# A zeroed tile shared on GpSimd, one VectorE instruction folded, and six semaphores taken back by SyncE in the kernel's ending

## The chip, the cores and the metric

The kernel runs on one core of a Trainium2 chip. The time is the device time in microseconds (us). A kernel was executed three times or more on one chip, in rounds shared with the kernel before. Absolute times of different chips are not compared closely: ratios are of the same rounds.

The **span** runs from the first to the last instruction of the kernel in the trace. **Time minus span** is what is counted beyond it. Exact spans (to a nanosecond) come from the one profiled execution of a kernel. For its other executions the span is known to 0.1 us.

## The reference, cut to what matters

One token through attention over a window of 4096 cached keys and values, a dense GELU layer, and a gate between the two:

```python
def reference(A_x, A_k_cache, A_v_cache, A_wq, A_wo, B_x, B_w1, B_b1, B_w2, B_b2, gate_w):
    x = A_x
    g = _sigmoid((x * gate_w).sum(-1, keepdims=True))
    a = _A_ref(x, A_k_cache, A_v_cache, A_wq, A_wo)     # 32 query heads, 16 key heads, Dh = 128
    b = _B_ref(x, B_w1, B_b1, B_w2, B_b2)               # 576 -> 4608 -> 576
    return g * a + (1 - g) * b
```

Every weight and cached value is read once, 53.6 MB in all.

## The kernel before: the parts concerned

GpSimd makes constants at the opening, each with a memset and one or more selections:

```python
    perm = const.tile([P, 4, 4, 32], BF16, name="perm")
    nc.gpsimd.memset(perm[:], 0.0)
    nc.gpsimd.affine_select(out=perm[:], in_=perm[:], ...)            # cut
    hi5 = const.tile([P, 5], FP32, name="hi5")
    nc.gpsimd.memset(hi5[:], 1.0)                                     # two selections follow, cut
    lo31 = const.tile([P, RW], BF16, name="lo31")
    nc.gpsimd.memset(lo31[:], 0.0)
    for a in range(5):
        nc.gpsimd.affine_select(out=lo31[:], in_=lo31[:], pattern=[[-1, RW]], ..., base=-RW * a, ...)
    om_t = const.tile([P, 64], BF16, name="om_t")
    nc.gpsimd.memset(om_t[:], 0.0)
    wo_tail = const.tile([48, 4, D], BF16, name="wo_tail")
    nc.gpsimd.memset(wo_tail[:].bitcast(FP32), 0.0)
```

VectorE scales the softmax sums (`rgh` for four columns, `rgt` for the fifth), and TensorE folds the heads with `lo31`:

```python
    nc.vector.tensor_tensor(out=rgh[:], in0=rg[:].to_broadcast([P, Hq, 4]), in1=gh[:, :, 0:4]..., op=ALU.mult)
    nc.vector.tensor_scalar(out=rgt[:], in0=rg[:, :, 0], scalar1=gh[:, 0, 4:5], ...)
    # cut
    ov_mm = nc.tensor.matmul(ov_ps[:, 0:RO], lhsT=om[:]..., rhs=lo31[:], start=True, stop=True)
```

The ending is written by the kernel itself. SyncE issues the store, arrives at the kernel's barrier, waits until the store has landed and takes its semaphore back to zero. GpSimd waits for the loads' semaphores and four arrivals, then clears the other semaphores as two ranges:

```python
        last = copy.replace(leave, sync_info=mybir.SyncInfo(on_wait=[landed], on_update=[taken]))
        kept = [arrive, last]                  # SyncE: arrive, then wait for the store and take back
        # ACT, PE and DVE arrive, cut
        kept += [copy.replace(ours[0], sync_info=others), ours[1]]   # GpSimd: others' waits; 4 arrivals
        # two range clears, (lo, sem) and (sem + 1, hi), cut
```

## Time and profile before

| | before |
|---|---|
| time, median of the first three executions | 132.34 us (132.33 to 132.4) |
| span of the profiled execution | 130.28 us |
| its time | 132.28 us, so time minus span is 2.00 us |
| one load queue, share of 16 engines | 96.5% |

How to read it: the busy shares (TensorE 62%, VectorE 41%, GpSimd 8%) are no guide here, as the load queue is nearly always full. One looks for what can starve that queue, and for what stands behind its last byte. The prediction below shows the DMA rows and the end of the chain. The lines here are those that the parts of the change touch.

GpSimd's opening, from the timeline (start, length, engine, line, operation):

```profile
9.89 0.74 POOL L226 TENSOR_SCALAR_AFFINE_SELECT perm<-perm 128x512 bf16<-128x512 bf16 x1
10.76 1.05 POOL L271 MEMSET wo_tail<- 48x1152 f32 x1
...
14.79 1.56 POOL L291 TENSOR_SCALAR_AFFINE_SELECT foreign<-foreign 4x512 bf16<-4x512 bf16 x1
16.33 0.21 POOL L259 TENSOR_SCALAR_AFFINE_SELECT lo<-lo 128x31 bf16<-128x31 bf16 x1
16.50 0.99 POOL L384 MEMSET qz_flat<- 128x1084 f32 x1
```

GpSimd is done with its last constant at 17.5 us; nothing of it runs later but the ending.

VectorE at the softmax sums, same view; the bracket gives the idle time before an instruction and what ended it:

```profile
105.28 0.36 DVE L633 RECIPROCAL rg<-mt_ps 128x32 f32<-128x32 f32 x1 [15.54 <-PE mt_ps L628]
105.68 0.29 DVE L635 TENSOR_TENSOR rgh<-rg,gh 128x128 f32<-128x128 f32 x1
105.89 0.23 DVE L642 TENSOR_SCALAR rgt<-rg,gh 128x32 f32<-128x32 f32 x1
114.89 0.29 DVE L661 TENSOR_TENSOR om<-o_ps,rgh 128x128 bf16<-128x128 f32 x1 [8.76 <-PE o_ps L603]
```

After `rgt` VectorE idles for 8.76 us. An instruction fewer here saves no waiting.

TensorE behind the folding products, and the very end:

```profile
121.89 2.61 PE L359 MATMUL y_ps<-wo_t,ov 128*1 128x288 bf16 x40 [0.19 <-DMA wo_t<-in_A_wo_dram]
125.35 1.39 PE L359 MATMUL y_ps<-w_t,gt 128*1 128x288 bf16 x20 [0.85 <-DMA w_t<-in_B_w_dram]
...
128.62 0.45 DVE L702 CAST out_row<-y_ps 1x288 bf16<-1x288 f32 x1 [11.72 <-PE y_ps L359]
129.12 0.28 SPq L703 DMA_DIRECT2D out_dram<-out_row  x1
```

TensorE waits for loads three times in the last 10 us (0.19, 0.85 and, at 127.44, 0.33 us), so a product more is taken in. The store's issue at 129.12 us is the last thing that these views show.

### The profile page before, as it was taken

To read this page: it belongs to the slowest core of one execution; us is meant where nothing else is said; L and a number is where in the kernel's file an instruction comes from. 1 tells how busy PE (TensorE), PEld (TensorE's weight loads), DVE (VectorE), ACT (ScalarE), POOL (GpSimd) and SP (SyncE) were. 2 spreads that over 40 slices of the span, in tenths; PEclk is the share of its full clock that TensorE was granted. 3 is DMA by queue.
4 is the path that set the end of the run, shared out by engine and by line. 5 is a ranking of instruction groups with operands and counts; after the bars stand their busy time and mean duration, and the time that the engine had idled before them with its cause. 6 is when DMAs were issued, how large, how long until landed. Compare 5 with 4: busy or idle time off the path is not lost.

```text
span 130.3 us, 2411 instructions
## 1 busy us (share of the span) xinstructions
PE 80.7 (62%) x1145; PEld 46.1 (35%) x1077; DVE 53.7 (41%) x49; ACT 8.3 (6%) x18; POOL 10.1 (8%) x34
## 2 busy tenths in 40 slices
PE   0036999476003998949909995985300930899973
PEld 0036949475000121202201121685300920864641
DVE  0056100300079969999999995604000020010001
ACT  3000000003000000030003003021000000000001
POOL 5029930000000000000000000000000000000000
PEclk9999999999999999999996899975555555555999
DMA  7999999899999899899999999899999999999980
GB/s 232 421 436 439 468 401 498 363 463 438 392 448 463 372 453 483 372 443 473 392 433 463 412 412 463 376 444 473 397 423 448 423 407 421 430 427 421 403 354 25
DMA packets 2508, 53.75 MB, mean 413 GB/s; under 512 B 286, under 2 KB 290, under 8 KB 580
## 3 DMA queue, kind: packets, MB, share of 16 engines
q1 hardware_dynamic: 2490, 53.61, 96.5%
q8 instruction: 8, 0.13, 0.4%
q10 hardware_dynamic: 10, 0.01, 0.0%
HBM read 53.62 MB, written 0.00 MB: 412 GB/s over the span
## 4 chain that ended last, share of the span: by engine, by line
DMA 52%; DVE 24%; PE 14%; issue 6%; SPq 2%
DMA k_t<-in_A_k_cache_dram 27%; DMA w_t<-in_B_w_dram 25%; DVE kt L494 19%; PE s_ps L516 7%; PE o_ps L603 5%; DVE m L532 3%; DVE pt L565 2%; PE y_ps L359 1%; SPq L651 1%; DVE mr L535 1%; SPq L658 0%; SPq L194 0%; PE mt_ps L541 0%; DVE out_row L702 0%; SPq L190 0%
## 5 line engine op out<-in xcount | busy, mean ns | idle before, releaser
L516 PE MATMUL s_ps<-kt,qz_flat 128*128 128x512 bf16 x128 | 32.6, 412 | 17.2 <-DVE kt L494 10.4
L494 DVE STREAM_TRANSPOSE kt<-k_t 128x4096 f32<-128x4096 f32 x8 | 35.3, 4432 | 11.7 <-DMA k_t<-in_A_k_cache_dram 10.3
L603 PE MATMUL o_ps<-pt,v_t 128*128 128x8 bf16 x512 | 14.2, 167 | 16.8 <-DMA v_t<-in_A_v_cache_dram 14.8
L516 PEld LDWEIGHTS <-qz_flat 128*128 128x128 bf16 x64 | 6.8, 107 | 40.3 <-issue 40.2
L603 PEld LDWEIGHTS <-v_t 128*128 128x128 bf16 x512 | 14.1, 102 | 17.5 <-DMA v_t<-in_A_v_cache_dram 15.1
L387 PEld LDWEIGHTS <-w_t 128*128 128x128 bf16 x162 | 10.2, 165 | 0.9 <-issue 0.9
L387 PE MATMUL h_ps<-x,w_t 128*128 128x2 bf16 x162 | 10.4, 202 | 0.0
L359 PE MATMUL y_ps<-w_t,gt 128*1 128x288 bf16 x72 | 7.2, 363 | 1.2 <-DMA w_t<-in_B_w_dram 1.2
L553 ACT ACTIVATE p_t<-s_ps,negm 128x1024 bf16<-128x1024 f32 x4 | 4.5, 1113 | 50.9 <-DVE negm L549 50.9
L633 DVE RECIPROCAL rg<-mt_ps 128x32 f32<-128x32 f32 x1 | 0.4, 358 | 15.5 <-PE mt_ps L628 15.5
L565 DVE STREAM_TRANSPOSE pt<-p_t 128x1024 bf16<-128x1024 bf16 x4 | 4.9, 1224 | 2.7 <-ACT p_t L553 2.7
L425 PE MATMUL q_ps<-x,wq_t 128*128 128x2 bf16 x144 | 4.0, 166 | 2.7 <-DMA wq_t<-in_A_wq_dram 2.7
L702 DVE CAST out_row<-y_ps 1x288 bf16<-1x288 f32 x1 | 0.4, 445 | 11.7 <-PE y_ps L359 11.7
L308 PE MATMUL xs_ps<-one_b,rows 1*128 1x1 bf16 x9 | 0.7, 195 | 7.4 <-DVE rows L302 7.4
L532 DVE TENSOR_REDUCE m<-s_ps 128x1 f32<-128x1024 f32 x4 | 4.8, 1196 | 1.1 <-PE s_ps L516 1.1
L359 PEld LDWEIGHTS <-gt 128*1 128x1 bf16 x72 | 3.7, 99 | 3.6 <-issue 1.6
L425 PEld LDWEIGHTS <-wq_t 128*128 128x128 bf16 x144 | 3.9, 104 | 2.8 <-DMA wq_t<-in_A_wq_dram 2.8
L396 DVE COPY hacc<-h_ps 128x36 f32<-128x36 f32 x1 | 0.2, 196 | 10.6 <-PE h_ps L387 10.6
L359 PE MATMUL y_ps<-wo_t,ov 128*1 128x288 bf16 x62 | 4.3, 286 | 0.2 <-DMA wo_t<-in_A_wo_dram 0.2
L661 DVE TENSOR_TENSOR om<-o_ps,rgh 128x128 bf16<-128x128 f32 x1 | 0.3, 292 | 8.8 <-PE o_ps L603 8.8
L302 DVE COPY rows<-rows 1x1152 bf16<-1x1152 bf16 x1 | 0.7, 748 | 6.5 <-DMA rows<-in_A_x_dram 6.5
L359 PEld LDWEIGHTS <-ov 128*1 128x1 bf16 x62 | 2.6, 83 | 1.8 <-issue 0.8
(77 smaller groups left out, 39.1 us busy)
## 6 DMA issues: line engine op xcount, KB each, us to landing
k_t<-in_A_k_cache_dram SPq DMA_DIRECT2D x4, 4096.0 KB, 31.8
v_t<-in_A_v_cache_dram SPq DMA_DIRECT2D x4, 4096.0 KB, 23.2
wq_t<-in_A_wq_dram SPq DMA_DIRECT2D x1, 4608.0 KB, 25.8
w_t<-in_B_w_dram SPq DMA_DIRECT2D x1, 2880.0 KB, 14.2
w_t<-in_B_w_dram SPq DMA_DIRECT2D x1, 2592.0 KB, 23.1
w_t<-in_B_w_dram SPq DMA_DIRECT2D x1, 2304.0 KB, 8.1
wo_t<-in_A_wo_dram SPq DMA_DIRECT2D x1, 2304.0 KB
wo_t<-in_A_wo_dram SPq DMA_DIRECT2D x1, 2160.0 KB
```

What stands on the lines that cost most here:

```text
L302: nc.vector.tensor_copy(out=xdup.rearrange("p (d t) -> p d t", t=2), in_=x_row.rearrange("p (d o) -> p d o", o=1).to_broadcast([1, D, 2]),)
L359: last = nc.tensor.matmul(y_out[s], lhsT=vec, rhs=row[:, s * DH : (s + 1) * DH], start=start, stop=stop, skip_group_check=True,)
L387: nc.tensor.matmul(h_ps[:, j:NF:NJ], lhsT=w1_t[:, i, j:FH:NJ], rhs=x2[:, i, :], start=False, stop=(i == NI - 1 and j == NJ - 1), skip_grou ...
L425: nc.tensor.matmul(q_ps[:, j : Hq : Hq // 2], lhsT=wq_t[:, i, j * Dh : (j + 1) * Dh], rhs=x2[:, i, :], start=(i == 0 and j == 0), stop=(i ...
L494: lambda: nc.vector.transpose(out=kt[g, f][:].bitcast(FP32), in_=keys.rearrange("p c d -> p (c d)").bitcast(FP32),),
L516: last = nc.tensor.matmul(s_ps[g][:, u * 512 : (u + 1) * 512].rearrange("p (c k) -> p c k", k=32), lhsT=qz(g, j, 2 * f + half), rhs=kv[:, ...
L532: queue("dve", lambda: nc.vector.reduce_max(out=m1[:], in_=s_ps[g][:], axis=AX.X))
L535: lambda: nc.vector.tensor_scalar(out=mr[:], in0=hi16[:], scalar1=m1[:, 0:1], scalar2=None, op0=ALU.mult),
L553: nc.scalar.activation(out=p_t[:].rearrange("p c k -> p (c k)"), in_=s_ps[g][:], func=ACT.Exp, bias=negm[:, 0:1], scale=SCALE, accum_out=s ...
L565: lambda: nc.vector.transpose(out=pt[:, g, :, :].rearrange("p c q -> p (c q)"), in_=p_t[:].rearrange("p c k -> p (c k)"),),
L603: last = nc.tensor.matmul(o_ps[:, 8 * g : 8 * g + 8, 0], lhsT=v_t[g][:, c, :], rhs=pt[:, g, c % 32, 8 * (c // 32) : 8 * (c // 32) + 8], st ...
L651: nc.sync.dma_start(out=wo_t[:, r0:r1, :].rearrange("p r n -> p (r n)"), in_=wo_src[:, 0 : 4 * RW, :].rearrange("h (a r) n -> h a (r n)", ...
```

## The change

Intent: GpSimd zeroes one tile and cuts `perm`, five selections (now side by side, one instruction), `om_t` and `wo_tail` out of it. VectorE makes `rgh` five columns wide and drops `rgt`. TensorE adds up four products where `lo31` needed one. In the ending SyncE takes six semaphores back while its store flies, so GpSimd needs to wait for three arrivals only, and clears six semaphores where it cleared eleven (five of SyncE's six were among these).

```diff
+        first = min(w.id for w in store.sync_info.on_wait)
+        mine = [w for w in waits if w.id >= first and w.id != sem]
+        mine.append(...)                       # PE's semaphore, its value counted from the program; cut
+        mine.append(next(w for w in waits if w.id == sem))
+        waits = [w for w in waits if w.id < first]
-        kept = [arrive, last]
+        kept = []
+        for w, name in zip(mine, names):       # six: wait for w, take it back; no arrival
+            kept.append(copy.replace(leave, name=name, sync_info=mybir.SyncInfo(on_wait=[w], on_update=[taken])))
-        kept += [copy.replace(ours[0], sync_info=others), ours[1]]
+        kept += [copy.replace(ours[0], sync_info=others), copy.replace(ours[1], sync_info=three)]
-        for n, (a, b) in enumerate(((lo, sem), (sem + 1, hi))):
+        for n, (a, b) in enumerate(((lo, first), (stop, hi))):
 ... (cut)
-    perm = const.tile([P, 4, 4, 32], BF16, name="perm")
-    nc.gpsimd.memset(perm[:], 0.0)
+    zeros = const.tile([P, NZ + 4 * D], BF16, name="zeros")
+    nc.gpsimd.memset(zeros[:].bitcast(FP32), 0.0)
+    # perm, at31, om_t and wo_tail are parts of zeros; one selection fills at31 (cut)
-    nc.gpsimd.memset(hi5[:], 1.0)
-    # lo31: memset and five selections; memsets of om_t and wo_tail (cut)
 ... (cut)
-    rgh = const.tile([P, Hq, 4], FP32, name="rgh")
+    rgh = const.tile([P, Hq, 5], FP32, name="rgh")
-    rgt = const.tile([P, Hq], FP32, name="rgt")
-    nc.vector.tensor_scalar(out=rgt[:], in0=rg[:, :, 0], scalar1=gh[:, 0, 4:5], ...)
 ... (cut)
-    ov_mm = nc.tensor.matmul(ov_ps[:, 0:RO], lhsT=om[:]..., rhs=lo31[:], start=True, stop=True)
+    for a in range(4):
+        ov_mm = nc.tensor.matmul(ov_ps[:, 0:RO], lhsT=om[:]..., rhs=at31[:, a, :], start=(a == 0), stop=(a == 3))
```

## The prediction

> **What bounds the kernel now.** I read the page's slices first, then the queues, the chain of work that ended last, and the timeline of the last microseconds; after that the semaphore records that the trace keeps beside the instructions, because the change is about semaphores and no page counts those as work.
>
> ```profile
> DMA  7999999899999899899999999899999999999980
> GB/s 232 421 436 439 468 401 498 363 463 438 392 448 463 372 453 483 372 443 473 392 433 463 412 412 463 376 444 473 397 423 448 423 407 421 430 427 421 403 354 25
> ...
> q1 hardware_dynamic: 2490, 53.61, 96.5%
> ```
>
> The last four pieces of the chain that ended last (start, length, what):
>
> ```profile
> 94.31 33.08 DMA w_t<-in_B_w_dram
> 127.39 0.04 issue
> 127.44 1.19 PE y_ps L359 x16
> 128.62 0.43 DVE out_row L702
> ```
>
> The DMA row is at 8 or 9 tenths in every slice from the second to the last but one, and one queue is busy for 96.5% of sixteen engines' span. So the run is one unbroken load of 53.6 MB with a tail behind it. The second fence ends in that tail: the last products, then the two copies of the result.
>
> Does any load wait for GpSimd or VectorE work? The loads' issue times against their sizes answer it. When VectorE lets the third value block be issued, at 79.60 us, the earlier issues add up to 36,960 KB, or 37.8 MB. At the mean of 413 GB/s, 79.6 us have moved 32.9 MB. So 4.9 MB, 12 us of transfer by my estimate, are still queued; the other late issues leave more (6.5 MB at 86.47 us). **No engine that is made 2 us quicker or 1 us slower in the middle moves the end of the stream.** What is left is what stands behind the last byte.
>
> **The end, from the trace's records.** The last load's semaphore is complete at 128.07 us, and the copies end at 129.04 (ScalarE) and 129.06 (VectorE). SyncE issues the store from 129.12 to 129.40, arrives at the kernel's own barrier at 129.67, and takes the store's semaphore back at 130.28, because the store has landed at 130.25. GpSimd waits for four arrivals, the last being SyncE's at 129.67, passes at 129.71, clears two ranges of semaphores, and ends at 130.09. The span ends there with SyncE, at 130.28, yet the profiled run is counted at 132.28 us. The missing 2.0 us are in the records of semaphore 2: nine increments at 128.903, 129.231, 130.621, 130.666, 130.689, 130.786, 130.826, 130.860 and 130.906[...], then nine more increments from 131.715 to 132.072.
>
> [...] two rounds of nine increments, steps of 23 to 98 ns where nobody is late, and ranges of 51 (54 to 104, 105 to 155, 156 to 206). [...] The increment at 128.903 can only be TensorE's, which alone had ended by then. [...] The range 105 to 155 is zeroed in groups of four every 21 to 22 ns, the rhythm in which GpSimd clears 99 to 109 inside the kernel (129.903, 129.925, 129.946). So **the third position is GpSimd**, and SyncE is the fifth.
>
> Read so, the first round says who is late: positions 4 and 5 follow the third by 45 and 23 ns, exactly as in the second round (44 and 24 ns), so they had been ready. The program's end now waits for GpSimd, which reports 0.527 us after its last clear (130.621 minus 130.094), and not for SyncE, although SyncE's is the last instruction of the span.
>
> [...] Here, on the hardware queue, issue to landing of the store is 1.13 us (129.12 to 130.25)[...]. [...] On GpSimd [...] 1084 fp32 in 991 ns and 512 bf16 in 522 ns, 0.91 and 1.02 ns each. So zeroing bf16 through a 4-byte view halves the cost.
>
> **The change part by part.**
>
> *GpSimd's opening.* Removed are the memsets of perm (0.52 us), lo31 (0.13), om_t (0.15), wo_tail (1.05) and hi5 (0.11) and five selections of lo31 (5 x 0.21 = 1.05): 3.0 us. Added are one memset of 1518 4-byte elements (1518 x 0.91 = 1.4 us) and one selection of 155 columns (estimate from perm's: 0.745 x 155/512 = 0.23, say 0.3 us). Net about 1.3 us of GpSimd work gone; and as the large memset runs before 9.05 us, where GpSimd idles for 6.7 us, qz_flat may be ready some 2 us sooner than 17.5 us. TensorE waits for it about 1 us and would finish the hidden layer's first half earlier, at most 1 us. Then it waits for wq as it does now (2.7 us until 27.0). **Worth 0.**
>
> *VectorE.* The 0.235 us of rgt go, and rgh grows from 128 to 160 columns (estimate 0.29 x 160/128, plus 0.07 us). This lies at 105 to 106 us, before 8.8 us of waiting for the last value products. **Worth 0.**
>
> *TensorE.* One product with lo31 becomes four that add up: three more of 0.1 to 0.2 us, near 116.4 us, up to 0.6 us later. Behind them TensorE waits for loads at 121.89 (0.19 us), 125.35 (0.85 us) and 127.44 us (0.33 us). The sum, 1.37 us, takes that in. **Worth 0.**
>
> *SyncE and GpSimd at the end.* SyncE no longer arrives at the barrier; it takes five semaphores back before the store's. Each such record lasts 0.02 us, and its neighbours start 0.05 to 0.08 us apart, so I take five at 0.07 = 0.35 us from 129.46, done by 129.8, before the landing at 130.25. Hidden. GpSimd now needs three arrivals, the last at 129.116 instead of 129.671, and clears six semaphores instead of eleven in its first range: it passes at 129.16, ends 0.38 us later at 129.54 (five fewer at 5 ns save 0.025, which I round away), and reports at 129.54 + 0.527 = 130.07, 0.55 us sooner.
>
> The round cannot gain all of that: SyncE still ends at 130.28 and stands fifth. How long it takes from its last record to its increment is not shown. TensorE takes 0.245 us (128.658 to 128.903), ScalarE 0.159 (129.072 to 129.231); SyncE at most 0.406 (130.689 minus 130.283). With 0.2 us, it reports at about 130.48 instead of 130.689. **Gain 0.2 us, between 0 and 0.4**, and everything behind the fifth increment moves by the same. Sum: 132.34 - 0.2 = 132.14 us, or 0.15% less.
>
> **Rivals.** First: *SyncE already sets the end* (its position is the third and my reading of the rhythm is wrong). The span's own last instruction speaks for it, the equal steps of the two rounds against the idea that both are near. Then the gain is 0: 132.3 us. Second: *the wait moves on to SyncE and grows*. If each take-back were to cost 0.2 us instead of 0.07, as its drain in this kernel lasts (0.207), five end at 130.46, past the landing, and the end gets 0.2 us later than the above: 132.3 to 132.4. Third: *the quicker start pays after all*, about 1 us, 131.3. The 4.9 MB that are always queued speak against it. Fourth: a wo_tail load or a product that is delayed by the shared zeroed tile, whose writers are now tied together: the load waits on a GpSimd count reached before 20 us and is issued at 80.2, so nothing.
>
> **Range and chances.** The unprofiled runs lie within 0.07 us. The gain's own limits, 0 and 0.4 us, give 131.94 to 132.34; a run-to-run 0.05 above gives the upper edge. Two per cent would be 2.6 us, more than the whole part behind the kernel's last instruction. Only a cause that I do not see would reach it.
>
> **What would show it.** In the changed kernel: the last load complete within 0.1 us of 128.07; the store issued near 129.1; GpSimd's last clear near 129.5, before the store lands; SyncE's fifth take-back before 130.0; the third increment of semaphore 2 no longer the late one, but the fifth, at 130.4 to 130.6; the span unchanged at about 130.3 while the time falls by 0.2. An unchanged gap of 0.34 us from SyncE's end to the late increment would show the first rival right, take-backs beyond 130.25 the second, a stream that ends sooner the third. The prediction is wrong if the stream itself shifts by more than 0.3 us, for a reason such as other addresses of the tiles, or if the five-engine order is not what I inferred.

What rested on no trace or run of this case is cut from the prediction; the cuts are marked. No term of its sum is among them: 132.34 less 0.2 makes the 132.14 us. What has lost its ground is the step from the records to the order of the engines. That the third increment is GpSimd's and the fifth SyncE's was the estimate at that time, with one rhythm to speak for it (groups of four semaphores every 21 to 22 ns, in the range 105 to 155 as in GpSimd's own clears). The later runs bear the two out, as told below. "Is zeroed" stands for what the trace shows between the two rounds of increments: one update of each of the semaphores 7 to 255, in five ranges, from 130.82 to 131.63 us. These records do not give the value written. That zeroing through a 4-byte view halves the cost is an estimate from the two memsets quoted.

## The result, and the profile after

| | before | after |
|---|---|---|
| time, median of four | 132.34 us (132.31 to 132.4) | 131.65 us (131.53 to 131.88) |
| ratio of the means, 95% interval | | 0.995, 0.9933 to 0.9967 |
| span of the profiled execution | 130.28 us | 130.11 us |
| time minus span, profiled | 2.00 us | 1.42 us |

A ratio here is the mean time of one kernel's fast runs over that of the other's of the same rounds, so not quite the ratio of the medians. The gain is 0.5%, within the two per cent that count as the same, clear of the noise, and **over three times what was predicted**: 131.65 lies below the range of 131.94 to 132.4. In a repeat on another chip (experiment 9) the medians differed by 0.52 us.

The load stream of the kernel after, DMA rows of the page:

```profile
DMA  6999999799899999999899899899899899999980
...
q1 hardware_dynamic: 2490, 53.61, 96.5%
```

The chain that ended last, its last pieces:

```profile
94.29 32.93 DMA w_t<-in_B_w_dram
127.22 0.04 issue
127.27 1.19 PE y_ps L396 x16
128.45 0.43 DVE out_row L736
```

Nothing has changed in kind. The span is shorter by 0.17 us in this pair of executions, but over its four executions it read 130.1, 130.2, 130.3 and 130.5 us, and before's seven on another chip 130.1 to 130.4. So no move of the stream is seen. The parts of the change inside the span did what was expected of them. GpSimd after:

```profile
1.86 1.36 POOL L267 MEMSET zeros<- 128x1518 f32 x1
...
10.29 0.59 POOL L281 TENSOR_SCALAR_AFFINE_SELECT zeros<-zeros 128x155 bf16<-128x155 bf16 x1
...
14.47 0.99 POOL L421 MEMSET qz_flat<- 128x1084 f32 x1
```

The new memset took 1.36 us (1.4 was predicted), the selection 0.59 (0.3; 0.37 in pool_work), and the last memset ends 2.0 us sooner than before. VectorE after:

```profile
105.77 0.33 DVE L672 TENSOR_TENSOR rgh<-rg,gh 128x160 f32<-128x160 f32 x1
114.72 0.29 DVE L694 TENSOR_TENSOR om<-o_ps,rgh 128x128 bf16<-128x128 f32 x1 [8.63 <-PE o_ps L640]
```

The wider `rgh` costs 0.04 us, `rgt` is gone, and the wait of 8.6 us stays. TensorE and the end after:

```profile
121.72 2.61 PE L396 MATMUL y_ps<-wo_t,ov 128*1 128x288 bf16 x40 [1.42 <-DMA wo_t<-in_A_wo_dram]
125.18 1.39 PE L396 MATMUL y_ps<-w_t,gt 128*1 128x288 bf16 x20 [0.84 <-DMA w_t<-in_B_w_dram]
...
128.44 0.45 DVE L736 CAST out_row<-y_ps 1x288 bf16<-1x288 f32 x1 [11.62 <-PE y_ps L396]
128.96 0.28 SPq L737 DMA_DIRECT2D out_dram<-out_row  x1
```

From the copies to the store's issue it is the same 0.5 us. So **the gain lies behind the span**, and the page cannot show it: 2.00 us fell to 1.42. What can show it are the trace's records of semaphore updates and of DMA transfers, which reach past the last instruction of the kernel. The instructions of the kernel name semaphores 96 to 110, none of them semaphore 2. From 128.7 us on the trace has eighteen updates of it, in two rounds of nine (the increments), in us from the span's start:

```
before, first round   128.903 129.231 130.621 130.666 130.689 130.786 130.826 130.860 130.906
after,  first round   128.731 129.062 129.863 129.907 130.250 130.294 130.333 130.367 130.413
before, second round  131.715 131.749 131.787 131.831 131.855 131.953 131.991 132.026 132.072
after,  second round  131.198 131.232 131.270 131.462 131.485 131.583 131.621 131.655 131.702
```

Whose an increment is, no record says; they are named by what they follow. In both traces the first comes 0.245 us after TensorE's last drain, the second 0.159 us after ScalarE's last record and the third 0.527 us after GpSimd's last clear. The fifth comes 0.137 or 0.138 us after SyncE's last record in all fourteen runs with the new ending. The fourth and the sixth are taken for VectorE's by elimination and by what experiments 5 and 6 do to them.

Between the rounds the trace has one update each of semaphores 7 to 255 (249 records before; 230 after, where some are missing). The texts call this zeroing. The range 156 to 206 is taken for VectorE's, since its start moves with VectorE's number of records: 0.545 to 0.555 us after the sixth increment in the four runs with 59, 0.135 or 0.136 in the thirteen with fewer, 0.697 in the one with 60. The sixth increment is therefore called VectorE's release, and the extra time a stall.

Four things are to be seen.

1. The third increment (GpSimd's) comes 0.527 us after GpSimd's last clear in both kernels (130.094 and 129.336). Before, the fourth and fifth follow it by 0.045 and 0.023 us, as in the second round (0.044 and 0.024), so it was the late one. After, the fifth (SyncE's) is late: 0.343 us after the fourth, and 0.137 us after SyncE's last record at 130.113. That is as predicted.
2. VectorE's range, 156 to 206, began at 131.331 before and 130.429 after: 0.545 us and 0.135 us after the sixth increment. A stall of 0.41 us has gone from there. By itself it cost nothing that shows: the second round's first increment comes 0.255 us (before) and 0.225 us (after) after the end of another range, 7 to 53 (131.460 and 130.973), and before, the fourth increment followed the third in 0.044 us.
3. In the second round after, the fourth increment follows the third by 0.192 us in place of 0.044: it is late here now.
4. Before, one DMA transfer of 8192 bytes that the trace marks as "instruction" stands at the very end, from 132.033 to 132.564 (the late fetch, below). After, there is none.

Where does counting stop? Before, the time (132.28) is the end of that fetch less 0.28. After, it is the ninth increment less 0.17. The experiments show whether this holds in other runs.

### The profile page after: what moved, and what is told of

It reads as the page before. It is cut to its first block, busy times and chain, and to the rows that moved or that the text cites. A ratio compares the mean times of both kernels' runs of the same rounds, so it can differ in the third digit from the quotient of the medians.

```text
span 130.1 us, 2403 instructions
## 1 busy us (share of the span) xinstructions
PE 79.7 (61%) x1148; PEld 45.6 (35%) x1077; DVE 52.3 (40%) x48; ACT 8.3 (6%) x18; POOL 9.2 (7%) x26
## 3 DMA queue, kind: packets, MB, share of 16 engines
q1 hardware_dynamic: 2490, 53.61, 96.5%
## 4 chain that ended last, share of the span: by engine, by line
DMA 52%; DVE 24%; PE 14%; issue 6%; SPq 2%
DMA k_t<-in_A_k_cache_dram 27%; DMA w_t<-in_B_w_dram 25%; DVE kt L531 19%; PE s_ps L553 7%; PE o_ps L640 5%; DVE m L569 3%; DVE pt L602 2%; PE y_ps L396 1%; SPq L684 1%; DVE mr L572 1%; SPq L691 0%; DVE out_row L736 0%; SPq L234 0%; SPq L230 0%; PE mt_ps L578 0%
## 5 line engine op out<-in xcount | busy, mean ns | idle before, releaser
L396 PE MATMUL y_ps<-w_t,gt 128*1 128x288 bf16 x72 | 6.3, 329 | 1.2 <-DMA w_t<-in_B_w_dram 1.2
```

Of the source, the lines that this page charges most:

```text
L396: last = nc.tensor.matmul(y_out[s], lhsT=vec, rhs=row[:, s * DH : (s + 1) * DH], start=start, stop=stop, skip_group_check=True,)
```

## The experiments

First theory (the prediction's): the new ending is all that counts. Rival: about half comes from shorter instruction streams. "Records" below are the instructions of an engine in the trace: VectorE has 59 before and 58 after, GpSimd 60 before and 46 after. All kernels gave correct results. The records of all runs stand in one table after the single accounts.

**1. The ending alone (a_end).** The kernel before with the changed `store_ends_program`:

```diff
-        kept = [arrive, last]
+        kept = []            # six waits with take-backs, three arrivals, ranges (lo, first), (stop, hi)
```

> Kernel before with the new ending alone (SyncE takes six semaphores back, GpSimd waits for three arrivals); its GpSimd and VectorE programs stay as long as they were. Theory of the prediction (the ending is all that counts, the rest of the measured gain is part of it too): about 131.65 us, time minus span 1.4 us as in the changed kernel, against 2.0 before. Rival (about half comes from shorter instruction streams): the third barrier increment comes 0.53 us after GpSimd's last clear, early, and the fifth sets the round, 0.14 us after SyncE's end, but VectorE still starts zeroing its range about 0.5 us after its release and an 8192-byte instruction fetch still stands at the end; time minus span 1.6 to 1.8, so 131.9 to 132.1 us.

Measured: 131.74 us against 132.25, ratio 0.9966 (0.9951 to 0.9981), time minus span 1.43 in the profiled execution and 1.43 to 1.54 in four. The ending alone brings most of the gain. But VectorE still starts zeroing 0.545 us after its release, and a fetch stands at the end (131.781 to 132.123). So the rival's signs are there, while the first theory's number is nearly met and the rival's (1.6 to 1.8) is missed. The fetch was short in this execution, 0.34 us against 0.53 before. As all four executions read 1.54 or less, that is not the luck of one of them; why it is short is not shown.

**2. The programs alone (b_prog).** The changed kernel with the old `store_ends_program`:

```diff
-        kept = []            # six waits with take-backs, three arrivals
+        kept = [arrive, last]            # and four arrivals, ranges (lo, sem), (sem + 1, hi)
```

> Changed kernel with the old ending: shorter GpSimd and VectorE programs alone. Theory of the prediction (opening and middle are hidden): 132.3 us, time minus span 2.0. Rival (shorter instruction streams count): the third increment stays 0.53 us after GpSimd's last clear, which again waits for SyncE, but VectorE starts zeroing 0.1 to 0.2 us after its release instead of 0.55, only six of the eight 8192-byte instruction fetches are left, and time minus span is 1.6 to 1.8, so 131.9 to 132.1 us.

Measured: 131.98 us against 132.25 on the same chip, ratio 0.9981 (0.9966 to 0.9996), time minus span 1.73, fetch gone, VectorE's zeroing 0.135 us after its release. **The first theory falls**: the programs that it gave no worth are worth about 0.27 us (2.00 to 1.73) with the old ending. The rival's numbers are met. With equal programs, the ending is then worth 1.73 to 1.42, that is 0.32 us.

**3. VectorE's one instruction put back (c_rgt).**

```diff
+    rgt = const.tile([P, Hq], FP32, name="rgt")
+    nc.vector.tensor_scalar(out=rgt[:], in0=rg[:, :, 0], scalar1=gh[:, 0, 4:5], scalar2=None, op0=ALU.mult)
```

> Changed kernel with VectorE's one removed instruction (rgt) put back, so its program is as long as before. Theory (one instruction of 0.23 us in idle time is nothing): same as the changed kernel, 131.65 us, time minus span 1.4. Rival [...]: VectorE's zeroing starts 0.5 us after its release again, the late instruction fetch is back, 0.3 to 0.4 us slower, about 132.0 us.

The cause that the rival named is cut; no run shows it. Measured: 131.84 us, time minus span 1.64 (1.48 to 1.7 in four). The stall of 0.555 us before the zeroing is back, and so is the late fetch. An instruction of 0.23 us, which ran in 8.8 us of idle time 25 us before the end, costs about 0.2 us behind the end here (1.64 against 1.42). With GpSimd's old opening it costs less: a_end, as long on VectorE, read 1.43 to 1.54, and end_v (experiment 8), one instruction shorter, 1.37 to 1.45.

**4. Fourteen tiny memsets on GpSimd (d_pool14), and a large one three times (pool_work).**

```diff
+    pad = const.tile([1, 2], FP32, name="pad")
+    for _ in range(14):
+        nc.gpsimd.memset(pad[:], 0.0)
```

> Changed kernel with fourteen tiny memsets of GpSimd added at its opening, so its program is again as long as before. Theory (the opening is hidden): same as the changed kernel, 131.65 us. Rival [...]: 0.3 to 0.4 us slower, about 132.0 us, with one instruction fetch of 8192 bytes more than the changed kernel has.

The cause that the rival named is cut here too. Measured: 132.28 us, ratio 1.0 (0.9983 to 1.0017), time minus span 1.92. The whole gain is lost, with a fetch from 132.165 to 132.583. Its control adds work instead of instructions:

```diff
     nc.gpsimd.memset(zeros[:].bitcast(FP32), 0.0)
+    nc.gpsimd.memset(zeros[:].bitcast(FP32), 0.0)
+    nc.gpsimd.memset(zeros[:].bitcast(FP32), 0.0)
```

> Changed kernel with the large zeroing memset of GpSimd done three times: 2.8 us more GpSimd work, as much as or more than the fourteen tiny memsets cost, but only two instructions more. If the number of instructions made that run 0.6 us slower, this one is as the changed kernel: time minus span 1.42, no instruction fetch at the end. If it was the work at the opening, this one is slower too, time minus span 1.9, or a later end of the stream.

From the timeline of pool_work:

```profile
1.87 1.37 POOL L267 MEMSET zeros<- 128x1518 f32 x1
...
9.86 1.36 POOL L268 MEMSET zeros<- 128x1518 f32 x1
...
12.11 1.35 POOL L269 MEMSET zeros<- 128x1518 f32 x1
...
16.76 1.57 POOL L330 TENSOR_SCALAR_AFFINE_SELECT foreign<-foreign 4x512 bf16<-4x512 bf16 x1
```

GpSimd's opening now ends at 18.3 us, later than in the kernel before. Measured: 131.69 us, ratio 0.9956, time minus span 1.42, no late fetch. So on GpSimd it is **the number of instructions, not the work**, that counts here (1.92 with fourteen tiny memsets more, 1.42 with two large ones).

**5. VectorE shorter by one, two and three (dve_m1, dve_m2, dve_m3).** Small operations of the gate go to GpSimd: the add to `ge`, then also `omg`, then also `b2g` and `gh`.

```diff
-    nc.vector.tensor_scalar(out=ge[:], in0=ge[:], scalar1=1.0, scalar2=None, op0=ALU.add)
+    nc.gpsimd.tensor_scalar(out=ge[:], in0=ge[:], scalar1=1.0, scalar2=None, op0=ALU.add)
     # dve_m2: omg too; dve_m3: b2g and gh too
```

> Changed kernel with the add of 1 to ge moved from VectorE to GpSimd: VectorE's program one instruction shorter, GpSimd's one longer. Theory A (VectorE meets one stall of 0.4 to 0.55 us at a fixed place of its instruction stream, one code place later for each instruction removed; in the changed kernel it lies between the end of its zeroing and its increment in the second round): the stall moves behind that increment, so fourth follows third by 0.04 us again, and VectorE's way-back increment, the sixth, comes about 0.4 us late; time minus span about 1.7 us, slower by 0.3. Theory B (the stall has nothing to do with length): as the changed kernel, time minus span 1.42, fourth 0.19 us after third.

Measured: 131.59 us, ratio 0.9949 (0.9934 to 0.9964), time minus span 1.29. The stall nearly vanished from both rounds: fourth after third 0.055, sixth after fifth 0.109 us. Theory A expected it behind the increment already, and a loss of 0.3; so its step was off by one.

> As the run with one instruction less, and omg moved to GpSimd too: VectorE two instructions shorter than in the changed kernel. Theory A: the stall lies behind VectorE's last increment, the second round takes its bare 0.36 us instead of 0.50, and time minus span is about 1.27 us if nothing of VectorE's counts after that, so 131.5 us and the best so far; up to 1.7 if VectorE's own end is counted. Theory B: 1.42.

Measured: 131.99 us, time minus span 1.70. The fourth follows in 0.044 us, but the sixth, also taken for VectorE's, comes 0.530 us after the fifth instead of 0.098. That is what theory A expected one instruction earlier. For this run it gave 1.27, or up to 1.7 were VectorE's own end counted: 1.70 came, but from the sixth increment.

> As the run with two instructions less, and b2g and gh moved to GpSimd too: VectorE three instructions shorter than in the changed kernel, GpSimd five longer. Theory A: no stall inside either round, bare 0.36 us, time minus span at most 1.27 us, 131.5 us. Theory B: 1.42.

Measured: 132.08 us, time minus span 1.67. Both rounds are bare (0.36 us for the second), as theory A said, yet the time is not less: it stops 0.22 us after the ninth increment. The late part may lie behind VectorE's last increment, where no record shows it; that is not shown. So the late place moves on as VectorE's program gets shorter: the start of its range with 59 records (0.545 us in place of 0.135), the fourth increment of the second round with 58 (0.192 in place of 0.044), hardly any with 57 (0.055, and 0.109 for the sixth), the sixth of that round with 56 (0.530 in place of 0.098). "At most 1.27" was a miss.

**6. VectorE longer (dve_p2).** The changed kernel with `rgt` computed three times; the build merged one wait, so VectorE has 60 records, two more than changed and one more than before.

```diff
+    for _ in range(3):
+        nc.vector.tensor_scalar(out=rgt[:], in0=rg[:, :, 0], scalar1=gh[:, 0, 4:5], scalar2=None, op0=ALU.mult)
```

> Changed kernel with rgt put back and one repetition more of it: VectorE two instructions longer than in the changed kernel, one longer than before. Theory A: the stall moves one place further ahead, to before VectorE's release or its increment in the first round; zeroing then starts 0.135 us after the release, the first round's sixth increment may come up to 0.15 us late, and the fetch at the end stays. Time minus span 1.6 to 1.8. Rival (only the length before counted, by chance): as the changed kernel, 1.42.

Measured: 131.86 us, time minus span 1.55. The late fetch stays, but earlier (131.416 to 131.909). The stall before the zeroing did not move ahead. It grew to 0.697 us, and the fourth increment is late as well (0.184 us). The simple picture of one stall that wanders one place per instruction fails in this direction.

**7. VectorE's part alone, GpSimd's part alone (v_only, g_only)**, each on the kernel before with the old ending; g_only has the four products too, which go with the tile.

```diff
 v_only:
-    rgh = const.tile([P, Hq, 4], FP32, name="rgh")         # and rgt
+    rgh = const.tile([P, Hq, 5], FP32, name="rgh")
 g_only:
-    perm, lo31, om_t, wo_tail: a memset each, five selections for lo31
+    nc.gpsimd.memset(zeros[:].bitcast(FP32), 0.0)          # and one selection for at31
```

> Kernel before with VectorE's part alone (rgh five columns wide, rgt gone): VectorE one instruction shorter, GpSimd as long as before, old ending. Theory A (VectorE's stall moves past its zeroing and its fetch at the end goes): VectorE's zeroing starts 0.135 us after its release. If nothing else is late, time minus span is 1.73 as in the run with both programs short and the old ending. Theory C (GpSimd's length of 60 records brings its own late fetch, as the fourteen memsets did): a fetch starts about 0.2 us after the ninth increment, time minus span 2.1 to 2.2, no gain at all, so VectorE's part needs GpSimd's.

Measured: 132.53 us, ratio 1.0031 (1.0011 to 1.0051), time minus span 2.31, a fetch from 132.297 to 132.790. Its span gives no hint. First line of its page:

```profile
span 130.2 us, 2410 instructions
```

VectorE's part alone is **slower** than the kernel before. Theory C is met in kind; its 2.1 to 2.2 us were 0.1 to 0.2 too low.

> Kernel before with GpSimd's part alone (one zeroed tile, one selection, four products in place of one), VectorE as long as before, old ending. Theory A: VectorE's stall before its zeroing (0.55) and its late fetch stay, time minus span 1.9 to 2.0, as before: 132.2 us. If GpSimd's length alone counted: 1.73.

Measured: 132.26 us, ratio 1.0001, time minus span 2.00. GpSimd's part alone is worth nothing either; VectorE's stall (0.555) and fetch stay. Under the old ending only both together give the 0.27 us.

**8. Where GpSimd's limit lies (pool12, pool13, end_v).** end_v is the kernel before with the new ending and VectorE's part, without any shared tile; the other two are d_pool14 with fewer memsets.

```diff
-    for _ in range(14):
+    for _ in range(12):      # pool13: range(13)
```

> Changed kernel with twelve instead of fourteen tiny memsets of GpSimd: 58 GpSimd records, as many as the kernel before with the new ending has, which showed no fetch of GpSimd's own. If the late fetch of GpSimd has a threshold between 58 and 60: as the changed kernel, time minus span 1.42. If every instruction costs: 1.85. If the threshold is lower: 1.9.

Measured: 131.83 us, 58 records, no late fetch in the profiled execution, time minus span 1.42; in four 1.39, 1.47, 1.98, 1.39.

> Changed kernel with thirteen tiny memsets: 59 GpSimd records. Twelve gave 1.39 to 1.47 in three executions and 1.98 in one, fourteen 1.89 to 1.97 in all. If the limit is a count: all near 1.42 or all near 1.95. If near the limit it falls out by chance: a mixture, more of the slow ones than with twelve.

Measured: 132.27 us, 59 records, a fetch from 132.217 to 132.541, time minus span 1.6 to 2.04 in six, median 1.9. So the limit lies between 58 and 59 records for most executions: one of four was slow below it, and one of six read only 1.6 above it.

> Kernel before with the new ending and VectorE's part, but GpSimd's old opening: no shared zeroed tile at all. GpSimd has 58 records (60 less the two that the ending saves). If GpSimd's part works only by its length with a limit between 58 and 60: as the changed kernel, time minus span 1.42, in some executions 1.95. If the zeroed tile does something of its own: 1.7 or more in all.

Measured: 131.73 us against 132.26, time minus span 1.42 in the profiled execution and 1.37 to 1.45 in all six. **The shared zeroed tile is not needed**, and the four products in place of one cost nothing that shows, as end_v has neither: the new ending saves GpSimd two instructions, and that brings it from 60 to 58 records.

**9. The best version against the changed kernel on one chip (after_again, m1_again).**

> The changed kernel once more, as the mark for the others on this chip: time minus span 1.38 to 1.43, about 0.6 us under the kernel before.

> The changed kernel with VectorE one instruction shorter still (add of 1 to ge on GpSimd), the best so far: time minus span 1.27 to 1.32, so 0.1 us under the changed kernel on the same chip, if the stall's place is a matter of VectorE's length; the same as the changed kernel if the earlier 0.1 was another chip's.

Measured: the changed kernel 131.74 us, ratio 0.9967 (0.9946 to 0.9988); time minus span 1.43, 1.45, 2.02, 1.45, 1.73 and 1.44. The version with the add on GpSimd: 131.60 us, ratio 0.9949 (0.9934 to 0.9964); time minus span 1.24 to 1.32 in four. The intervals overlap, so the time alone does not part the two; time minus span does, by some 0.15 us in the medians. This version beats the kernel before clearly, and the changed kernel slightly and in time minus span alone. That two of six executions of the changed kernel ran 0.3 and 0.6 us longer behind the same sort of span was not expected. It was not seen in its first four.

All profiled executions side by side. "SyncE" is the fifth increment less SyncE's last record. "Zeroing" is the first update in the range 156 to 206 less the sixth increment. "4-3" and "6-5" are steps of the second round. "Fetch" is the end of the late fetch less the ninth increment. "Count" is the time less the end of the late fetch, or less the ninth increment in brackets where there is none.

```
run          VectorE GpSimd ending  SyncE  zeroing  4-3    6-5    fetch  count    time - span
before          59     60    old    0.406   0.545  0.044  0.098   0.492  -0.284     2.00
v_only          58     60    old    0.403   0.136  0.192  0.099   0.686  -0.290     2.31
g_only          59     48    old    0.415   0.555  0.045  0.098   0.497  -0.291     2.00
b_prog          58     48    old    0.406   0.135  0.188  0.097   none  (-0.179)    1.73
a_end           59     58    new    0.137   0.545  0.052  0.097   0.279  -0.293     1.43
c_rgt           59     46    new    0.137   0.555  0.052  0.098   0.492  -0.294     1.64
after           58     46    new    0.137   0.135  0.192  0.098   none  (-0.172)    1.42
end_v           58     58    new    0.138   0.136  0.191  0.100   none  (-0.178)    1.42
pool12          58     58    new    0.138   0.135  0.193  0.098   none  (-0.180)    1.42
pool13          58     59    new    0.138   0.136  0.192  0.098   0.525  -0.291     1.83
d_pool14        58     60    new    0.137   0.135  0.160  0.098   0.624  -0.293     1.92
pool_work       58     48    new    0.137   0.135  0.163  0.099   none  (-0.180)    1.42
dve_m1          57     47    new    0.137   0.136  0.055  0.109   none  (-0.171)    1.29
dve_m2          56     48    new    0.137   0.136  0.044  0.530   none  (-0.177)    1.70
dve_m3          55     51    new    0.137   0.136  0.044  0.097   none  (0.221)     1.67
dve_p2          60     46    new    0.138   0.697  0.184  0.098   0.259  -0.289     1.55
after_again     58     46    new    0.138   0.135  0.205  0.099   none  (-0.172)    1.43
m1_again        57     47    new    0.138   0.135  0.044  0.101   none  (-0.175)    1.30
```

The column "count" settles where counting stops: in all eight runs with a late fetch, the time is the fetch's end less 0.28 to 0.29 us, and in nine of the ten without, it is the ninth increment less 0.17 to 0.18 (the tenth is dve_m3). **In these eight executions the late fetch of 8192 bytes sets the end of the time.** In the eighteen profiled executions it appears exactly when VectorE has 59 records or more, or GpSimd 59 or more. Before, with both over the limit, it comes where VectorE's does (it starts 0.08 us after the sixth increment of the second round; 0.04 to 0.06 in g_only, c_rgt and a_end) and not where GpSimd's does (0.31 to 0.33 us after it in v_only, pool13 and d_pool14). That is why v_only is slower than before: the later fetch is the one left (it ends 0.686 us after the ninth increment, against 0.492). Why GpSimd's fetch is not late there is not explained.

## Why the prediction was wrong, point by point

*The stream is the bound, and nothing in the middle moves its end.* Right. The load queue kept its 96.5%, and the spans of both kernels cover the same 130.1 to 130.5 us.

*GpSimd's opening: "Worth 0".* Right for this change, but its working counts only work. As work it is worth nothing, as pool_work shows with 2.7 us more of it. As a count of instructions it can be worth something: from 58 to 59 records the time minus span rises by 0.4 us (1.42 in pool12, 1.83 in pool13, profiled). Here the new ending alone brings GpSimd to 58, so that the old opening does as well (end_v, 1.42).

*VectorE: "Worth 0".* **Failed.** The one instruction dropped takes VectorE's stall out of the place before its zeroing, and its late fetch away. With GpSimd also short, it is worth 0.27 us under the old ending (g_only to b_prog) and 0.22 under the new one (c_rgt to after). The working looked at durations and idle time, and these were right. That the number of an engine's instructions can bring a fetch behind the end did not come up.

*TensorE: "Worth 0".* Right, as far as was tested: end_v, with one product and without the tile, reads the same 1.42. The waits for loads behind the products stayed (1.42, 0.84 and 0.33 us after).

*SyncE's take-backs.* Right. The five before the store's lie between 129.289 and 129.612 us, 0.07 to 0.09 apart, and the store's take-back starts at 130.096.

*GpSimd third, SyncE fifth, and the wait passing from one to the other.* Right. GpSimd's last clear ended 0.10 us after the store's issue ended, instead of 0.69 us after, and still took 0.527 us to report.

*The ending: "Gain 0.2 us, between 0 and 0.4", and "everything behind the fifth increment moves by the same".* **This is the step on which the sum failed, in two ways.** First, it was mis-sized. I took 0.2 us for SyncE's way from its last record to its increment; it is 0.137 us. So the fifth comes 0.27 us sooner against SyncE's end (0.406 less 0.137). I also left out a step: where the third was the late one, the step from fifth to sixth took 0.097 us, and where the fifth is the late one it takes 0.044. Together 0.32 us, which is what the same programs show between the two endings (1.73 less 1.42).

Second, what lies behind the first round of increments did not move by the same. From its sixth increment to where the time stops it took 1.49 us before and 1.24 after. The late fetch is gone, so that the time stops 0.17 us before the ninth increment of the second round in place of 0.21 behind it (0.38 gained); VectorE's stall now lies inside that round (0.15 lost); the gap between the rounds is 0.03 shorter. That is 0.26 us which the prediction had no term for.

*The sum.* 0.32 and 0.26 make 0.58 us, the measured fall in time minus span (2.00 to 1.42). How much of it belongs to which part of the change has no single answer. The new ending takes time minus span from 2.00 to 1.43 with both programs long (before, a_end), from 2.31 to 1.42 with VectorE's short (v_only, end_v), from 2.00 to 1.64 with GpSimd's short (g_only, c_rgt), and from 1.73 to 1.42 with both short (b_prog, after). So the ending alone would have done nearly all of it (in the medians of a_end, 132.25 to 131.74), and the prediction gave it 0.4 us at most. The medians fell by 0.69; the rest must lie in the spans, of which the ones before are not on record for those rounds.

*The rivals.* SyncE as the end already: fell, by the increments. The wait growing on SyncE: fell. The quicker start: fell; the last load was complete 0.13 us sooner (127.94 against 128.07, a little over the 0.1 us allowed), not 1 us. The tied zeroed tile: no effect seen. None named the late instruction fetch.

**What stays open.** The records name neither the engine that a fetch is for nor its address, nor whose an increment of semaphore 2 is. That the fetches belong to VectorE and GpSimd is inferred from whose length brings them. That a stall is an engine's wait for instructions is not shown either: no fetch is on record during the stalls (none between 130.786 and 131.331 before). SyncE's stream has grown by four records with the new ending, which was not varied on its own. Why the stall grows in dve_p2 instead of moving, why in the changed kernel it costs 0.15 us in the second round, and why one of four executions of pool12 and two of six of after_again ran long, is not shown.

## What to carry to other kernels

This kernel ended some 2 us before its time did, and in that stretch the number of instructions on an engine counted where their work did not: dropping one VectorE instruction in idle time gained 0.27 us, nothing, or lost 0.31, by what else was in the kernel, and in most executions twelve GpSimd memsets were free while thirteen cost 0.4. When a change moves the time and not the span, compare time minus span, then the semaphore and fetch records behind the last instruction, and test with added instructions that do nothing as well as with added work. Try parts together: VectorE's part alone made this kernel slower; with GpSimd's part, or with the new ending, it did not.
